# Feed-forward weights narrowed in place; weight remainders and gate products dealt out anew between VectorE and GpSimd

## The chip, the cores and the metric

The kernel runs on one core of a Trainium2 chip. The metric is the device time of one execution, in microseconds (us). The engines are TensorE (PE in the profile, its weight loads PEld), VectorE (DVE), ScalarE (ACT), GpSimd (POOL) and SyncE (SP), which issues most transfers. Each has its own queue of instructions and works through it in a fixed order.

## The reference, cut to what matters

```python
def reference(**kwargs):
    attn_out = _attn_ref(q, k, v, tau)            # 4 batches, 8 heads, 576 tokens, 64 wide
    x = attn_out.transpose(0, 2, 1, 3).reshape(B * S, H * D)        # 2304 x 512
    x = _moe_ref(x=x, **moe_kwargs)               # 8 experts, w1 512 x 1024, w2 1024 x 512
    return _moe2_ref(x=x, **moe2_kwargs)

def _moe_ref(x, expert_emb, tau, w1, w2):
    ...
    for e in range(E):                            # each token goes to its best expert
        h = np.maximum(x[mask] @ w1[e], 0.0)
        out[mask] = gate_w[mask, None] * (h @ w2[e])

def _moe2_ref(x, w_in, w_out):                    # w_in 512 x 2048, w_out 2048 x 512, as float64
    h = x @ w_in
    sp = np.where(h > 20.0, h, np.log1p(np.exp(np.minimum(h, 20.0))))
    return (h * np.tanh(sp) @ w_out).astype(np.float32)
```

## The kernel before

**Stages.** The attention with the router fills the first 298 us. Then come eight visits, called experts 0 to 7 here (`visit`, L984), in which the tokens of an expert are gathered and go through its two products, up to about 565 us. The feed-forward runs in five groups of token columns (2, 4, 4, 4, 4 blocks) to the end.

**Split products.** Each f32 operand of a product is held as a high part, rounded to the type that TensorE takes, and a remainder. A product is three matmuls: high by high, low by high, high by low. So each operand costs a cast on ACT (`xh`, `wh`, `hi`) and a subtraction (`xl`, `wl`, `lo`). For the hidden tiles the subtraction is L1067 on DVE (`lo`), for the gathered rows L1044 on DVE (`xl`), for the experts' weights L960 (`wl`), on DVE or on POOL by the table `PR2['split']`. An expert's weights are four quarters of 128 x 2048 (`raw`, 1 MB each), and each quarter is cast and subtracted in two halves of 1024 columns.

**A visit.** `fetch` (L962) gathers 128 token rows with their gate from DRAM (L966, on POOL's queue) into one of three buffers `q32` and multiplies them by the gate, which stands in a column beside the row (on ACT at L971). PE transposes them (L1037), four matmuls each, with `ident`. The first product (L1061) makes eight hidden tiles u = 0 to 7, each with its `hi` and `lo`; the next expert's transposes stand between the seventh and the eighth tile. The second product (L1084) takes the `hi` and `lo` of all eight. The first expert's first 256 rows are done ahead of the rest (`early_part`), while `dispatch` and `places` (L773 to L879) work out where every token goes, in some 60 small operations on DVE.

**Narrowing.** The feed-forward's weights lie in DRAM as float64. `ffn_narrow` (L1208) turns them into f32 in 32 pieces of 128 x 512. A piece is loaded into `fraw` (512 KB, two buffers). ACT scales its high words into `b`. DVE makes in `c` the low word shifted right by 29 (L1221, the shift count being a second operand `by29`), puts the sign to it (L1222), then adds `b` shifted left by three (L1225). `c` (two buffers) is stored to DRAM. Before the feed-forward `ffn_weights` (L1239) reads the pieces back (L1251), casts them (L1253, ACT) and subtracts (L1257, DVE or POOL).

**What sets the order.** Every step is an operation of a planner (`Plan.add`), with an engine, an assumed duration, a priority (`prio`) and an assumed delay until its result can be used (`lat`). `Plan.order` simulates the engines by these numbers and writes down an order for each of them; the priorities come from the tables `PR` and `PR2`. An engine doesn't leave this order at run time: if the instruction at its head waits, all behind it wait.

Of the kernel before, what the change touches and what calls it, by code (L numbers as in the profile page):

```python
# [7 lines left out]
F32 = mybir.dt.float32  # L8
# [3 lines left out]
U32 = mybir.dt.uint32  # L12
# [24 lines left out]
PR = {'er': -15.54, 'ep': 12.91, 'ep2': 5.77, 'route': 119.01, 'route2': 74.91, 'rkpos': 41.48, 'rkpos2': 8.02, 'S': -59.65, 'max': -521.82, 'exp': 48.0, 'stt': -105.97, 'thr': 8.58, 'T': 9.58, 'Tp': 199.57, 'Tc': -0.63, 'TL': 10.76, 'TLp': 55.36, 'TLc': -285.26, 'pv': 19.05, 'x': -3.47, 'po': 66.46, 'osb': -13.34, 'px': 210.03, 'xev': 161.57, 'rd': 140.54, 'scale': 121.08, 'load': -59.04, 'xsc': 97.82, 'Ts': 2.12, 'xpos': 10.54, 'early': 270.81, 'h0': 16.86, 'h1': 9.87, 'h2': 34.96, 'h3': 47.14, 'rk3': 10.38, 'rk4': 11.04, 'tp3': 62.39}  # L37
PR2 = {'f0': (103, 153, 152, 184), 'pipe': (), 'dve_hi': (0, 5, 6), 'xo': 24.33, 'ps': (9.4, 19.4), 'cd': 1048576.0, 'split': (('ACT', 'DVE'), ('ACT', 'DVE'), ('ACT', 'POOL'), ('ACT', 'POOL'), ('ACT', 'DVE'), ('ACT', 'DVE'), ('ACT', 'POOL'), ('ACT', 'DVE')), 'sl': 28000, 'll': 2000, 'pool_lo': (0, 2, 5, 7), 'gbuf': 4, 'lag': 897.0, 'fw': 842.14, 'fw_act': (0, 1, 2, 3), 'fw_pool': (1, 3), 'n0': 0, 'n1': 0.46, 'np': 396.93, 'ld': -414.26, 'w0': -38.7, 'w1': -307.33, 'wlo': 327.12, 'xg': -219.77, 'xt': -641.51, 'xh': -523.34, 'h': -520.32, 'hs': -813.02, 'ht': -471.8, 'hh': -463.67, 'yy': -39.15, 'ye': 28.32, 'yi': 894.81, 'fy': 292.37, 'ft': 292.4, 'fx': 257.19, 'f1': -828.67, 'sg': -63.24, 'rc': 593.64, 'gg': 101.32, 'gh': -7.22, 'gl': -102.51, 'ob': -951.49, 'pt': -761.98, 'acc': 3.98}
# [212 lines left out]
class Kernel:  # L251
# [76 lines left out]
    def consts(self):  # L328
# [38 lines left out]
        self.by29 = c("by29", [128, 1], U32)  # L367
# [27 lines left out]
        def weights():  # L395
# [12 lines left out]
            g.iota(self.by29, pattern=[[0, 1]], base=29, channel_multiplier=0)  # L408
# [569 lines left out]
    def put(self, v, d, o, y, n, dst, prio, after):  # L978

        nc, add = self.nc, self.pl.add  # L980
        add("ACT", t_act(n), lambda: nc.scalar.copy(y()[:, 0:n], o()[:, 0:n]), r=[o], w=[y], prio=prio - 800)  # L981
        return add("SP", 600, lambda: nc.sync.dma_start(dst(), y()[:, 0:n]), r=[y, "off"], w=[("y", v, d)], prio=prio, lat=2000, dma=512.0 * n, after=after)

    def visit(self, v):  # L984
# [12 lines left out]
        for c in range(4):  # L997
# [7 lines left out]
            add("SP", 600, load, r=["reg"], w=[rt], prio=T - 200 + c if v else 100 + c, lat=2000, dma=PR2["cd"])  # L1005
# [19 lines left out]
        for k in range(k0, k0 + n):  # L1025
# [3 lines left out]
            self.fetch(self.ids[:, j:j + 1], self.x_dram[:, :], need, xg, -600 + T + 10 * k, "ACT")  # L1029
# [112 lines left out]
    def overflow(self, i):  # L1142
# [26 lines left out]
        R = [h("b", 0), h("b", 1), h("c", 0), h("c", 1)]  # L1169
# [38 lines left out]
    def ffn_narrow(self, n, i, at, raw, e, w, keys, after=()):  # L1208
# [5 lines left out]
        kr, ke, kw = keys  # L1214
        add("SP", 600, lambda: nc.sync.dma_start(raw(src.dtype), src[:, s]), w=[kr], prio=at - 4, lat=2000, dma=524e3, after=after)
# [43 lines left out]
    def ffn_rows(self, gi):  # L1259
# [223 lines left out]
```

## Time and profile before

| | |
|---|---|
| median of 3 runs | 988.83 us (988.18 to 992.61) |
| the profiled execution | 993.31 us |
| its span, first to last instruction | 991.6 us |
| PE busy | 926.2 us, 93% |
| DVE busy | 745.3 us, 75% |
| ACT busy | 569.3 us, 57% |
| POOL busy | 341.5 us, 34% |
| mean clock granted to PE | 0.979 |

The profile shows one execution. Busy time says how long an engine worked, not what the end waited for. For that one reads, stage by stage, how much PE lacks of the stage, which instructions ended its waits, and then what stood ahead of those instructions on their own engine. A row of waits sums the idle time of an engine just before an operation and names what released it. The granted clock is the share of TensorE's full speed in a stretch.

### The profile page before, as it was taken

The page shows a single profiled execution, that of the slowest core. Times are in us where ns is not written, and L with a number is a line of the kernel's source. Part 1 is how long each engine was busy: PE and PEld are TensorE (multiplying, and loading weights), DVE is VectorE, ACT ScalarE, POOL GpSimd, SP SyncE. Part 2 cuts the span into 40 slices and gives each one's busy share as a digit, 9 for nine tenths or more (in the row PEclk, how much of TensorE's full clock was granted, in tenths as well). Part 3 has the DMA queues.
Part 4 walks back from the last instruction along what each step waited for, and adds up shares of the span by engine and source line. Part 5 has one row for each costly group of instructions (what it writes and reads, how often), then busy time and mean ns, then how long its engine had stood idle before and what let it go on. Part 6 is the DMA issues. An engine that isn't in the chain of part 4 may idle for free. (4 is left out here: it accounts for less than half of the span.)

```text
span 991.6 us, 17464 instructions
## 1 busy us (share of the span) xinstructions
PE 926.2 (93%) x6574; PEld 740.6 (75%) x6574; DVE 745.3 (75%) x1023; ACT 569.3 (57%) x933; POOL 341.5 (34%) x429
## 2 busy tenths in 40 slices
PE   5899999999899898998989998999999999999997
PEld 3456555555568888998989996788888888888885
DVE  6888988888839586977894775994859495775972
ACT  3778887777765544555555673552635354443551
POOL 4333333333215222413333642332433233324223
PEclk7999999999999998999999899999999999999999
DMA  4122423323324778988878540100100001000001
GB/s 151 59 94 92 131 80 123 99 82 119 134 88 170 257 271 297 296 319 306 285 282 273 184 146 3 43 22 22 43 22 22 21 1 43 1 1 22 21 1 43
DMA packets 45637, 115.73 MB, mean 117 GB/s; under 512 B 11029, under 2 KB 16170, under 8 KB 41450
## 3 DMA queue, kind: packets, MB, share of 16 engines
q1 hardware_dynamic: 42426, 104.30, 31.2%
q0 software_dynamic: 3120, 10.25, 2.9%
q8 instruction: 54, 0.88, 0.4%
q14 instruction: 37, 0.30, 0.1%
HBM read 91.55 MB, written 22.97 MB: 115 GB/s over the span
## 5 line engine op out<-in xcount | busy, mean ns | idle before, releaser
L1340 DVE RECIPROCAL p<-p 128x512 f32<-128x512 f32 x72 | 241.0, 3347 | 100.6 <-ACT p L1336 100.6
L1345 POOL TENSOR_TENSOR lo<-p,hi 128x512 fp32r<-128x512 f32 x72 | 92.9, 1293 | 180.2 <-ACT hi L1344 101.1
L511 PE MATMUL D<-QK 64*128 64x288 f32 (+1 forms) x640 | 107.1, 457 | 21.1 <-DVE P L518 10.6
L517 ACT ACTIVATE E<-D,m 128x576 f32<-128x576 f32 x144 | 103.9, 742 | 37.3 <-DVE m L515 32.6
L515 DVE TENSOR_REDUCE m<-D 128x1 f32<-128x576 f32 x144 | 104.2, 750 | 16.2 <-PE D L511 16.0
L518 DVE SCALAR_TENSOR_TENSOR P<-D,thr,E 128x576 f32<-128x576 f32 x128 | 101.5, 812 | 15.0 <-ACT E L517 14.3
L960 POOL TENSOR_TENSOR wl<-raw,wh 128x1024 fp32r<-128x1024 f32 x24 | 62.7, 2628 | 107.1 <-ACT wh L958 106.6
L538 ACT COPY T<-D 128x1024 f32<-128x1024 f32 (+1 forms) x80 | 74.2, 929 | 29.4 <-PE D L535 28.8
L1344 ACT CAST hi<-p 128x512 fp32r<-128x512 f32 x72 | 44.0, 610 | 78.8 <-PE S L1352 42.6
L1084 PE MATMUL B<-lo,wh 128*128 128x256 f32 (+3 forms) x256 | 79.5, 311 | 8.6 <-DVE lo L1067 8.6
L516 POOL TENSOR_SCALAR thr<-m,ntau 128x1 f32<-128x1 f32 x144 | 38.6, 271 | 134.7 <-DVE m L515 116.9
L569 PE MATMUL D<-T,V 128*64 128x512 f32 x320 | 83.5, 608 | 0.9 <-DVE P L518 0.5
L1061 PE MATMUL S<-xh,wh 128*128 128x256 f32 (+3 forms) x256 | 78.7, 307 | 3.8 <-DVE lo L1067 3.6
L511 PEld LDWEIGHTS D<-QK 64*128 64x128 f32 (+1 forms) x640 | 47.2, 183 | 45.7 <-issue 18.4
L1084 PE MATMUL B<-hi,wh 128*128 128x256 f32 (+3 forms) x256 | 79.2, 309 | 1.5 <-ACT osb L981 0.9
L1061 PE MATMUL S<-xl,wh 128*128 128x256 f32 (+3 forms) x256 | 78.0, 304 | 2.4 <-DVE xl L1044 2.4
L1084 PE MATMUL B<-hi,wl 128*128 128x256 f32 (+3 forms) x256 | 78.8, 308 | 0.0
L1061 PE MATMUL S<-xh,wl 128*128 128x256 f32 (+3 forms) x256 | 78.1, 305 | 0.0
L958 ACT CAST wh<-raw 128x1024 fp32r<-128x1024 f32 x64 | 64.2, 1053 | 7.9 <-DMA raw<-in_wm_dram 4.0
L960 DVE TENSOR_TENSOR wl<-raw,wh 128x1024 fp32r<-128x1024 f32 x40 | 57.5, 1466 | 10.8 <-ACT wh L958 8.2
L1334 ACT ACTIVATE p<-S 128x512 f32<-128x512 f32 x36 | 21.5, 597 | 68.2 <-PE S L1326 52.1
L1084 PEld LDWEIGHTS B<-lo,wh 128*128 128x128 f32 x256 | 51.5, 201 | 10.1 <-DVE lo L1067 10.1
(296 smaller groups left out, 2308.4 us busy)
## 6 DMA issues: line engine op xcount, KB each, us to landing
raw<-in_wm_dram SPq DMA_DIRECT2D x32, 1024.0 KB, 7.9
QK<-in_qk_dram SPq DMA_DIRECT2D x32, 432.0 KB, 4.2
V<-in_v_dram SPq DMA_DIRECT2D x16, 512.0 KB, 3.2
fraw<-in_w_in_dram SPq DMA_DIRECT2D x16, 512.0 KB, 7.1
fraw<-in_w_out_dram SPq DMA_DIRECT2D x16, 512.0 KB, 5.0
x_dram<-xs SPq DMA_DIRECT2D x16, 256.0 KB
w_in_dram<-c SPq DMA_DIRECT2D x16, 256.0 KB
w_out_dram<-c SPq DMA_DIRECT2D x16, 256.0 KB, 5.3
```

The source lines that it names most:

```text
L511: nc.tensor.matmul(o, lhsT=QK()[r, a, q0:q0 + w], rhs=QK()[r, a, S:], start=True, stop=True)
L515: add("DVE", 680, lambda: nc.vector.tensor_reduce(m(), sv(), axis=AX.XY, op=ALU.max, negate=True), r=[sc], w=[m], prio=at + PR["max"])
L517: add("ACT", 660, lambda: nc.scalar.activation(Ev(), sv(), AF.Exp, bias=m(), scale=1.0), r=[sc, m], w=[E], prio=at + PR["exp"])
L518: add("DVE", 750, lambda: nc.vector.scalar_tensor_tensor(outs[0]().rearrange("p (a b) -> p a b", a=2), sv(), thr(), Ev(), op0=ALU.is_ge, o ...
L538: add("ACT", (2 * w + 100) / 1.2, lambda: nc.scalar.copy(T()[:, :, 0:w], pt()[:, :, 0:w]), r=[pt], w=[T], prio=at + PR["Tc"])
L569: mul = lambda j, o, c, rhs: nc.tensor.matmul(o, lhsT=V1()[:, c, :], rhs=rhs, start=(a == 0), stop=(a == 4))
L958: add("ACT", t_act(1024, False), lambda: nc.scalar.copy(hi()[:, s], raw()[:, s]), r=[kr], w=[kh], prio=prio, fill=fill)
L960: add(le, d, lambda: e.tensor_tensor(lo()[:, s], raw()[:, s], hi()[:, s].bitcast(F32), op=ALU.subtract), r=[kr, kh], w=[kl], prio=prio + . ...
L1061: hd(nc.tensor.matmul(hp(), lhsT=a()[:, kc, f], rhs=x()[:, kc, cols], start=(i == 0), stop=(i == 11)))
L1084: nc.tensor.matmul(o()[:, 0:N_], lhsT=w[a]()[:, u % 4, 128 * d:128 * (d + 1)], rhs=H2[x], start=(u == 0 and i == 0), stop=(u == 7 and i == 2))
L1340: v.reciprocal(q_(), q_())
L1345: add("POOL", t_pool(512), lambda q_=q_, gh=gh, gl=gl: g.tensor_tensor(gl(), q_(), gh().bitcast(F32), op=ALU.subtract), r=[q_, gh], w=[gl] ...
```

## The change

1. **Narrowing in place.** The shift writes back into `fraw` and takes its count as a number (one tensor operand). The sign is put to it there. The third operation writes into `b`, and `b` is what is stored. The tile `c` and the constant `by29` go; `b` has four buffers in place of two each of `b` and `c`, and where the feed-forward used two `b` and two `c` as result rows it uses four `b`. `fraw` is read until the third operation; before, the second was the last to read it.
2. **Remainders of the experts' weights** (`PR2['split']`, pairs for the two halves of quarters 0 to 3). Before, from the second expert on: DVE DVE, POOL POOL, DVE DVE, POOL DVE. After: POOL POOL, DVE DVE, DVE POOL, DVE POOL. The first expert's first quarter stays on DVE. In all 34 of the 64 on DVE, which had 40, and 30 on POOL, which had 24.
3. **Gate products of gathered rows**: on POOL for all experts but the first, 17 instructions of 128 x 512; before, all on ACT.
4. **The planner's numbers**: longer delays for the result store, the weight loads, the narrowing's loads and stores and the reading back, a shorter one between a stored piece and its reading, and some priorities. They change only the orders.

```diff
...
-'split': (('ACT', 'DVE'), ('ACT', 'DVE'), ('ACT', 'POOL'), ('ACT', 'POOL'), ('ACT', 'DVE'), ('ACT', 'DVE'), ('ACT', 'POOL'), ('ACT', 'DVE')), 'sl': 28000
+'split': (('ACT', 'POOL'), ('ACT', 'POOL'), ('ACT', 'DVE'), ('ACT', 'DVE'), ('ACT', 'DVE'), ('ACT', 'POOL'), ('ACT', 'DVE'), ('ACT', 'POOL')), 'sl': 2000
...
-            add("SP", 600, load, r=["reg"], w=[rt], prio=T - 200 + c if v else 100 + c, lat=2000, dma=PR2["cd"])
+            add("SP", 600, load, r=["reg"], w=[rt], prio=T - 200 + c if v else 100 + c, lat=7500 if v else 4000, dma=PR2["cd"])
...
-            self.fetch(self.ids[:, j:j + 1], self.x_dram[:, :], need, xg, -600 + T + 10 * k, "ACT")
+            self.fetch(self.ids[:, j:j + 1], self.x_dram[:, :], need, xg, -600 + T + 10 * k, "POOL" if v else "ACT")
...
-        R = [h("b", 0), h("b", 1), h("c", 0), h("c", 1)]
+        R = [h("b", x) for x in range(4)]
...
-        def low():
-            v.tensor_tensor(w(), words(U32, 0), self.by29.to_broadcast([128, 512]), op=ALU.logical_shift_right)
-            v.scalar_tensor_tensor(w(), words(U32, 1), 0x80000000, w(), op0=ALU.bitwise_and, op1=ALU.bitwise_or)
-
-        add("DVE", 690 + 690, low, r=[kr], w=[kw], prio=at)
-        add("DVE", 690, lambda: v.scalar_tensor_tensor(w(), e().bitcast(U32), 3, w(), op0=ALU.logical_shift_left, op1=ALU.bitwise_or), r=[ke], w=[kw], prio=at)
-        x = add("SP", 600, lambda: nc.sync.dma_start(self.f_dram[n][:, s], w().bitcast(F32)), r=[kw], w=[("f0", n, i)], prio=at, lat=2000, dma=262e3)
+        kt = (kr, "t")
+        add("DVE", 560, lambda: v.tensor_scalar(words(U32, 0), words(U32, 0), 29, None, op0=ALU.logical_shift_right), r=[kr], w=[kt], prio=at)
+        add("DVE", 690, lambda: v.scalar_tensor_tensor(words(U32, 0), words(U32, 1), 0x80000000, words(U32, 0), op0=ALU.bitwise_and, op1=ALU.bitwise_or), r=[kr, kt], w=[kt], prio=at)
+        add("DVE", 690, lambda: v.scalar_tensor_tensor(e().bitcast(U32), e().bitcast(U32), 3, words(U32, 0), op0=ALU.logical_shift_left, op1=ALU.bitwise_or), r=[kt, ke], w=[ke], prio=at)
+        x = add("SP", 600, lambda: nc.sync.dma_start(self.f_dram[n][:, s], e()), r=[ke], w=[("f0", n, i)], prio=at, lat=8000, dma=262e3)
...
```

Lines move up by two in `visit` and by four behind the narrowing, so that L1067 is L1065 after the change, L960 is L958, and L966 is L964. The orders of all engines are unchanged up to the end of the attention. Three places behind it follow.

On DVE, in the first product of expert 1, the second visit (128x384), where `lo` is the remainder of a hidden tile, `wl` that of the next expert's weights, and `c`, `fraw` and `b` belong to the narrowing. Before:

```order
L1067 SCALAR_TENSOR_TENSOR lo<-S,hi 128x384
L960 TENSOR_TENSOR wl<-raw,wh 128x1024 x2
L1067 SCALAR_TENSOR_TENSOR lo<-S,hi 128x384 x2
L1221 TENSOR_TENSOR c<-fraw,by_119 128x512
L1222 SCALAR_TENSOR_TENSOR c<-fraw,c 128x512
L1225 SCALAR_TENSOR_TENSOR c<-b,c 128x512
L1067 SCALAR_TENSOR_TENSOR lo<-S,hi 128x384
L1044 TENSOR_TENSOR xl_6791<-S,xh_6761 128x4x128 x3
L1221 TENSOR_TENSOR c<-fraw,by_119 128x512
L1222 SCALAR_TENSOR_TENSOR c<-fraw,c 128x512
L1067 SCALAR_TENSOR_TENSOR lo<-S,hi 128x384
```

After:

```order
L1221 SCALAR_TENSOR_TENSOR b<-b,fraw 128x512
L1065 SCALAR_TENSOR_TENSOR lo<-S,hi 128x384 x4
L1219 TENSOR_SCALAR fraw<-fraw 128x512
L1220 SCALAR_TENSOR_TENSOR fraw<-fraw 128x512
L1065 SCALAR_TENSOR_TENSOR lo<-S,hi 128x384
L1221 SCALAR_TENSOR_TENSOR b<-b,fraw 128x512
L1042 TENSOR_TENSOR xl_6766<-S,xh_6736 128x4x128 x3
L1219 TENSOR_SCALAR fraw<-fraw 128x512
L1220 SCALAR_TENSOR_TENSOR fraw<-fraw 128x512
L1065 SCALAR_TENSOR_TENSOR lo<-S,hi 128x384
```

The rows begin with the fourth `lo` before and with the third after. The pair of remainders behind the fourth `lo` went to another place, and four `lo`s now follow on each other. Ahead of the last `lo` two operations of the narrowing stand in both.

On POOL, at the gathers for experts 0 to 2; q32 with a number is one buffer's use, L964 the gather and L967 the gate product, L958 the remainder. Before:

```order
L966 DMA q32_5902<-x_dram_92,ids_156 128x514
L966 DMA q32_5909<-x_dram_92,ids_156 128x514
L966 DMA q32_5955<-x_dram_92,ids_156 128x514
L960 TENSOR_TENSOR wl_5830<-raw_5233,wh_5818 128x1024
L960 TENSOR_TENSOR wl_5988<-raw_5887,wh_5970 128x1024
L966 DMA q32_6025<-x_dram_92,ids_156 128x514
L966 DMA q32_6047<-x_dram_92,ids_156 128x514
L966 DMA q32_6056<-x_dram_92,ids_156 128x514
L966 DMA q32_6144<-x_dram_92,ids_156 128x514
L966 DMA q32_6173<-x_dram_92,ids_156 128x514
```

After:

```order
L964 DMA q32_5882<-x_dram_92,ids_155 128x514
L964 DMA q32_5894<-x_dram_92,ids_155 128x514
L964 DMA q32_5900<-x_dram_92,ids_155 128x514
L958 TENSOR_TENSOR wl_5908<-raw_5259,wh_5823 128x1024
L964 DMA q32_5994<-x_dram_92,ids_155 128x514
L967 TENSOR_SCALAR q32_5900<-q32_5900 128x512
L964 DMA q32_6031<-x_dram_92,ids_155 128x514
L964 DMA q32_6057<-x_dram_92,ids_155 128x514
L958 TENSOR_TENSOR wl_6028<-raw_5903,wh_6021 128x1024
L967 TENSOR_SCALAR q32_5994<-q32_5994 128x512
L964 DMA q32_6136<-x_dram_92,ids_155 128x514
L967 TENSOR_SCALAR q32_6031<-q32_6031 128x512
```

The gate products stand between the gathers now, one gather late: the product of q32_6031 comes behind the gather of q32_6136. The three buffers go round, so that this gather writes where q32_5994 was, whose transposes on PE stand directly ahead of those of q32_6031.

On DVE, in the first product of the last expert (128x192). Before:

```order
L960 TENSOR_TENSOR wl<-raw_8994,wh 128x1024 x2
L960 TENSOR_TENSOR wl<-raw,wh 128x1024
L1067 SCALAR_TENSOR_TENSOR lo<-S,hi 128x192 x4
L1257 TENSOR_TENSOR raw_9388<-raw_9388,raw 128x512
L1067 SCALAR_TENSOR_TENSOR lo<-S,hi 128x192
L1257 TENSOR_TENSOR raw_9388<-raw_9388,raw 128x512
L1067 SCALAR_TENSOR_TENSOR lo<-S,hi 128x192 x2
L1257 TENSOR_TENSOR wl<-wl,wh 128x512
L1067 SCALAR_TENSOR_TENSOR lo<-S,hi 128x192
```

After:

```order
L1065 SCALAR_TENSOR_TENSOR lo<-S,hi 128x192
L1253 TENSOR_TENSOR xl_9100<-xl_9100,xh_9182 128x512
L1065 SCALAR_TENSOR_TENSOR lo<-S,hi 128x192 x2
L1219 TENSOR_SCALAR fraw<-fraw 128x512
L1065 SCALAR_TENSOR_TENSOR lo<-S,hi 128x192
L1220 SCALAR_TENSOR_TENSOR fraw<-fraw 128x512
L1065 SCALAR_TENSOR_TENSOR lo<-S,hi 128x192
L1221 SCALAR_TENSOR_TENSOR b<-b,fraw 128x512
L1219 TENSOR_SCALAR fraw<-fraw 128x512
L1065 SCALAR_TENSOR_TENSOR lo<-S,hi 128x192
L1220 SCALAR_TENSOR_TENSOR fraw<-fraw 128x512
L1065 SCALAR_TENSOR_TENSOR lo<-S,hi 128x192
```

Before, no piece was narrowed here; now the narrowing's operations alternate with the `lo`s.

## Rows read from the trace of the kernel before

**Rows 1.** Stages: length; busy us of PE, PEld, DVE, ACT, POOL; clock, DMA share, GB/s.

```profile
298.00:345.00 47.00, 42.81 (x271) 38.47 (x271) 34.27 (x79) 24.47 (x42) 18.56 (x13) 0.96 0.58 211
345.00:545.00 200.00, 183.47 (x1255) 180.53 (x1254) 156.12 (x187) 109.19 (x184) 63.61 (x32) 0.97 0.85 291
545.00:625.00 80.00, 72.11 (x486) 64.98 (x485) 55.56 (x45) 44.50 (x85) 35.45 (x25) 0.94 0.35 110
625.00:992.00 367.00, 359.91 (x1565) 293.50 (x1563) 259.65 (x132) 170.58 (x288) 121.65 (x114) 0.99 0.06 21
```

**Rows 2.** PE's waits, 298 to 640 us: total us, times, longest.

```profile
PE B L1084 <- DVE lo L1067: 8.6, 5, 2.4
PE S L1037 <- DVE lo L1067: 4.3, 4, 2.1
PE S L1061 <- DVE lo L1067: 3.6, 2, 2.2
...
PE S L1061 <- DVE xl L1044: 2.4, 1, 2.4
...
PE S L1037 <- ACT q L971: 1.3, 1, 1.3
```

**Rows 3.** Stretches of 10 us with a lower granted clock, columns as in Rows 1.

```profile
320.00:330.00 10.00, 7.36 (x43) 6.77 (x42) 5.10 (x17) 2.83 (x7) 3.44 (x3) 0.83 0.87 323
370.00:380.00 10.00, 7.92 (x38) 7.82 (x38) 7.73 (x12) 4.39 (x7) 3.54 (x4) 0.83 1.00 376
380.00:390.00 10.00, 7.63 (x35) 7.42 (x34) 8.91 (x9) 4.08 (x8) 4.30 (x2) 0.83 0.64 185
...
530.00:540.00 10.00, 7.84 (x53) 7.63 (x52) 7.13 (x11) 5.69 (x11) 2.14 (x2) 0.83 0.83 292
```

**Rows 4.** Timeline 378 to 384 us: start, us, engine, line; in brackets idle before.

```profile
379.15 5.16 POOL L960 TENSOR_TENSOR wl<-raw,wh 128x1024 fp32r<-128x1024 f32 x2 [5.20 <-ACT wh L958]
...
379.32 2.75 DVE L1222 SCALAR_TENSOR_TENSOR c<-fraw,c 128x512 uint32<-128x512 uint32 x1
...
382.58 0.44 PE L1084 MATMUL B<-lo,wh 128*128 128x384 f32 x1 [2.37 <-DVE lo L1067]
```

**Rows 5.** Timeline 367 to 374 us, DVE and PE.

```profile
368.73 2.35 DVE L960 TENSOR_TENSOR wl<-raw,wh 128x1024 fp32r<-128x1024 f32 x2
...
372.08 0.66 PE L1037 MATMUL S<-ident,q 128*128 128x128 f32 x4 [2.11 <-DVE lo L1067]
```

**Rows 6.** DVE's groups from 298 us: busy us, mean ns, idle before by releaser.

```profile
L960 DVE TENSOR_TENSOR wl<-raw,wh 128x1024 fp32r<-128x1024 f32 x40 | 57.5, 1466 | 10.8 <-ACT wh L958 8.2 <-issue 2.6
L1222 DVE SCALAR_TENSOR_TENSOR c<-fraw,c 128x512 uint32<-128x512 uint32 x32 | 38.7, 1210 | 1.1
L1225 DVE SCALAR_TENSOR_TENSOR c<-b,c 128x512 uint32<-128x512 uint32 x32 | 27.2, 851 | 1.3
...
L1221 DVE TENSOR_TENSOR c<-fraw,by 128x512 uint32<-128x512 uint32 x32 | 26.0, 812 | 23.8 <-DMA w_in_dram<-c 12.9 <-DMA w_out_dram<-c 10.9
```

**Rows 7.** POOL's groups over the span, columns as in Rows 6.

```profile
L1345 POOL TENSOR_TENSOR lo<-p,hi 128x512 fp32r<-128x512 f32 x72 | 92.9, 1293 | 180.2 <-ACT hi L1344 101.1 <-PE S L1352 51.1 <-issue 12.0
L960 POOL TENSOR_TENSOR wl<-raw,wh 128x1024 fp32r<-128x1024 f32 x24 | 62.7, 2628 | 107.1 <-ACT wh L958 106.6 <-issue 0.5
...
L468 POOL TENSOR_SCALAR QK<-QK 128x288 f32<-128x288 f32 x31 | 28.9, 934 | 21.7 <-DMA QK<-in_qk_dram 18.6 <-PE D L535 3.0
```

**Rows 8.** Timeline 367 to 376 us, POOL.

```profile
371.10 0.94 POOL L966 DMA_INDIRECT q<-x_dram,ids  x1 [0.30 <-issue]
```

**Rows 9.** DVE's groups: a copy before, a PSUM operation after 298 us.

```profile
L450 DVE COPY EB<-ident 64x256 f32<-64x256 f32 x2 | 0.6, 284 | 0.0
...
L1341 DVE SCALAR_TENSOR_TENSOR p<-p,S 128x512 f32<-128x512 f32 x36 | 24.7, 687 | 1.5
```

**Rows 10.** Timeline 311 to 323 us, DVE and POOL.

```profile
313.26 5.33 DVE L863 TENSOR_TENSOR tl<-tl,ge 128x8 f32<-128x8 f32 x1
...
313.87 4.69 POOL L960 TENSOR_TENSOR wl<-raw,wh 128x1024 fp32r<-128x1024 f32 x2
```

More of the change, by code (lines that the diff above doesn't have):

```diff
@@ L38 @@
[L38 removed]
+PR = {'er': -15.54, 'ep': 12.91, 'ep2': 5.77, 'route': 119.01, 'route2': 74.91, 'rkpos': 41.48, 'rkpos2': 8.02, 'S': -59.65, 'max': -521.82, 'exp': 48.0, 'stt': -105.97, 'thr': 8.58, 'T': 9.58, 'Tp': 199.57, 'Tc': -3.64, 'TL': 10.76, 'TLp': 50.91, 'TLc': -285.26, 'pv': 19.05, 'x': -3.47, 'po': 66.48, 'osb': -13.34, 'px': 210.03, 'xev': 161.57, 'rd': 123.62, 'scale': 121.08, 'load': -59.04, 'xsc': 97.82, 'Ts': 2.12, 'xpos': 10.54, 'early': 245.34, 'h0': 16.86, 'h1': 9.87, 'h2': 34.96, 'h3': 30.12, 'rk3': 10.38, 'rk4': 11.53, 'tp3': 64.2}
@@ new lines @@
+PR2 = {'f0': (103, 154, 152, 184), 'pipe': (), 'dve_hi': (0, 5, 6), 'xo': 24.33, 'ps': (9.4, 19.4), 'cd': 1048576.0, 'split': (('ACT', 'POOL'), ('ACT', 'POOL'), ('ACT', 'DVE'), ('ACT', 'DVE'), ('ACT', 'DVE'), ('ACT', 'POOL'), ('ACT', 'DVE'), ('ACT', 'POOL')), 'sl': 2000, 'll': 2000, 'pool_lo': (0, 2, 5, 7), 'gbuf': 4, 'lag': 915.82, 'fw': 842.14, 'fw_act': (0, 1, 2, 3), 'fw_pool': (1, 3), 'n0': 0, 'n1': 0.46, 'np': 396.93, 'ld': -414.26, 'w0': -38.7, 'w1': -307.33, 'wlo': 327.12, 'xg': -219.77, 'xt': -641.51, 'xh': -523.34, 'h': -520.32, 'hs': -813.02, 'ht': -471.8, 'hh': -463.67, 'yy': -39.15, 'ye': 28.32, 'yi': 894.81, 'fy': 292.37, 'ft': 292.4, 'fx': 257.06, 'f1': -828.77, 'sg': -63.24, 'rc': 593.49, 'gg': 101.32, 'gh': -7.67, 'gl': -102.51, 'ob': -951.49, 'pt': -761.98, 'acc': 3.98}
@@ L981, in put @@
         add("ACT", t_act(n), lambda: nc.scalar.copy(y()[:, 0:n], o()[:, 0:n]), r=[o], w=[y], prio=prio - 800)
-        return add("SP", 600, lambda: nc.sync.dma_start(dst(), y()[:, 0:n]), r=[y, "off"], w=[("y", v, d)], prio=prio, lat=2000, dma=512.0 * n, after=after)
+        return add("SP", 600, lambda: nc.sync.dma_start(dst(), y()[:, 0:n]), r=[y, "off"], w=[("y", v, d)], prio=prio, lat=6000, dma=512.0 * n, after=after)
     def visit(self, v):
@@ L1155, in h @@
                 make = {"S": self.big, "B": self.bank}.get(kind, lambda at: self.row(kind, at))
-                if kind in "bc":
-                    make = lambda at: self.h("f", kind, [128, 512], F32 if kind == "b" else U32, 2, at)
+                if kind == "b":
+                    make = lambda at: self.h("f", "b", [128, 512], F32, 4, at)
                 keep[key] = make(at)
@@ L1204, in overflow, with ffn_narrow @@
         self.put_ids(self.idto[i:i + 1, :], lambda: self.id_dram[bass.ds(self.off, 128), :], K("idto"), T + 6)
-    def ffn_narrow(self, n, i, at, raw, e, w, keys, after=()):
+    def ffn_narrow(self, n, i, at, raw, e, keys, after=()):
         nc, add = self.nc, self.pl.add
@@ L1234, in narrow_late @@
             raw = self.h("f", "fraw", [128, 2 * YW], F32, 2, at)
-            e, w = self.h("f", "b", [128, 512], F32, 2, at), self.h("f", "c", [128, 512], U32, 2, at)
+            e = self.h("f", "b", [128, 512], F32, 4, at)
             j = x * PR2["n1"]
-            self.ffn_narrow(n, i, 200 + 10 * j + PR2["np"], lambda dt, raw=raw: raw()[:, 0:1024].bitcast(dt), e, w, [raw, e, w], [marks[min(int(j), SURE - 1)]])
+            self.ffn_narrow(n, i, 200 + 10 * j + PR2["np"], lambda dt, raw=raw: raw()[:, 0:1024].bitcast(dt), e, [raw, e], [marks[min(int(j), SURE - 1)]])
     def ffn_weights(self, n, c, at, tags):
@@ L1270, in ffn_rows @@
             X = [(self.row("hi", ah + .2 * x), self.row("lo", ah + .2 * x)) for x in range(2)]
-            X += [(h("f", "b", [128, 512], F32, 2, ah + x), h("f", "c", [128, 512], U32, 2, ah + x)) for x in range(2)]
+            X += [tuple(h("f", "b", [128, 512], F32, 4, ah + x + y) for y in (0, .5)) for x in range(2)]
         else:
```

9 lines of the change are left out of this document (3 added, 6 removed).

## The prediction

> **What bounds the kernel now.** I read first how busy each engine is by stage [rows 1]. In the last 367 us TensorE (PE) works 359.9 us, so nothing that the other engines save there can shorten it. In the three stages before, it lacks 4.2 of 47, 16.5 of 200 and 7.9 of 80 us, and no other engine is full: VectorE (DVE) is nearest with 156.1 of 200. So PE waits for single results, not for an engine's total. The view of PE's waits names them [rows 2]: 8.6 + 4.3 + 3.6 = 16.5 us end with DVE's `lo` (line 1067, the remainder of a hidden tile), 2.4 us with `xl` (line 1044), 1.3 us with the gate product on ScalarE (ACT, line 971). Third, the clock: in the stretches where PE had such a wait of some 2 us, the mean granted clock is 0.83 instead of 1 [rows 3], that is, a part of each at 1.2 instead of 2.4 GHz. A stretch of 10 us at 0.83 does 8.3 us of full-speed work, so each costs about 1.7 us beyond the wait: one such row in the first stage, three (5.1 us) in the second.
>
> Why is `lo` late? It is itself short. Two patterns stand ahead of it. One: two whole weight remainders (2.35 us) run on DVE just before `lo`, and PE waits 2.11 us [rows 5]. Two: POOL begins a pair of remainders at 379.15, DVE's second narrowing operation, started at 379.32, takes 2.75 us instead of 0.69, and `lo` behind it comes late; PE waits 2.37 us [rows 4]. An undisturbed DVE operation of that size with one tensor in PSUM takes 0.687 us [rows 9]. The five waits under B L1084 are mostly this second pattern, repeated in the next experts.
>
> **The change part by part.** The instruction orders are the same up to 298 us, and the work after 625 us is the same and bound by PE: 0 for both, and 0 for the constant that goes.
>
> *First experts, 298 to 345 us.* In the dispatch a DVE operation of 8 elements takes 5.33 us while POOL runs two remainders [rows 10]; the `xl` behind it are late and PE waits 2.4 us, with one slow stretch: 4.1 us together. After the change only one remainder stands between POOL's gathers there, and `xl` stands ahead of the last remainder on DVE, not behind it. That can free up to 4.1. Against it: on POOL the gate product of row q_6031 now stands behind the gather of q_6136, and that gather must wait until PE has transposed q_5994, whose buffer it takes. PE transposes q_5994 and q_6031 in one go. So PE waits for issue 0.30 + gather 0.94 [rows 8] + the gate product. No row shows this product on POOL. The lower end is POOL's subtraction of the same size, 1.29 us; a POOL multiplication by a per-row number over 288 columns takes 0.934, and by columns 512 would take 1.66; the upper end is the remainder of 1024 columns, 2.63 [rows 7]. I take 1.66, the nearest kind. The wait is 2.9 us (2.5 to 3.9) in place of the 1.3 [rows 2]: +1.6, and probably a slow stretch of 1.7. Net -4.1 + 1.6 + 1.7 = **-0.8** (from -2.9, with no slow stretch, to +4.3 with the dispatch wait still there). The later gate products have cover: a row gathered at 371.10 us [rows 8] goes into the buffer that the transposes of about that time have left, and is itself transposed only near the end of the next expert's first product, so I cost these products at nothing on PE; without that cover each costs up to its 1.66.
>
> *Experts 1 to 6, 345 to 545 us.* Six remainders leave DVE for POOL: 6 x 1.47 = 8.8 us less there [rows 6]. It matters where they stood: the order of DVE shows that the pair of remainders in the middle of expert 1's first product is gone from between its `lo`s. Pattern one should go. Pattern two is only half gone: the last `lo` of expert 1 still stands behind the first two narrowing operations; what changed is which quarter of the weights POOL takes, the first in place of the second, so its pair runs earlier, beside other DVE work. The narrowing's waits for its stores (12.9 + 10.9 us on DVE, the row of line 1221 in [rows 6]) were on DVE's queue but mostly before nothing urgent; longer latencies in the planner put them later. I take half of the 16.5 us: **-8** (from 0 to -14), and half of the slow stretches, **-2.5** (0 to -5.1).
>
> Of the narrowing itself: three operations per piece as before, 96 in all. The first has now one tensor in SBUF instead of two operands. Its price lies between twice a 256-column copy, 0.57 us [rows 9], and today's mean with disturbance, 0.812 [rows 6]; I take 0.69, which saves 32 x 0.12 = 4 us of DVE, part of the slack above and not a term of its own. In place, the raw buffer is held for one operation more, 0.7 to 0.85 us per piece and some more where that operation waits; the next load starts that much later, but the loads may now run on into expert 7, so I cost this at 0 for PE up to expert 6. The page "VectorE: DVE Perf Modes" of the Trainium skill (section "Mode 2×_2P") states that a one-source operation between SBUF tensors can run two elements per cycle; by it the shift would be near half of 0.69 and save a further 11 us of DVE, again off the path. No row of this kernel shows it at this size.
>
> *Last experts and the start of the feed-forward, 545 to 625 us.* The narrowing ended before expert 6; now some 10 of 32 pieces come after the first `lo` of expert 5, 6 of them among the `lo`s and remainders of experts 6 and 7. Six pieces are 18 x 0.69 = 12 us in a stage where DVE works 55.6 of 80 us [rows 1]. It fits by total, but each `lo` there may find one such operation ahead of it, and the feed-forward's weights are read back later. Today's PE loss there is 7.9 us; I take **+3** (0 to +8).
>
> Sum: -0.8 - 8 - 2.5 + 3 = **-8.3 us**. The profiled execution took 993.31 us (span 991.6), so it would be 985.0; the median of the runs is 988.83, 4.5 below the profiled one, and the forecast against it is 988.83 - 8.3 = **980.5 us**.
>
> **The rivals.** *The end gives it back (0.20).* The gains up to expert 6 are as above, but DVE is what the last two experts wait for: the +3 becomes its upper end +8, with one more slow stretch of 1.7. 980.5 + 5 + 1.7 = **987.2**. For it: half the DVE queue between the last `lo`s is narrowing now. Against: 55.6 + 12 of 80 is not full.
>
> *POOL stands in DVE's way (0.15, slower).* POOL gets 6 remainders (6 x 2.63 = 16 us) and 17 gate products (17 x 1.66 = 28 us) on top of 62.7 us of remainders [rows 7]. Today those 62.7 us stretch DVE's two-tensor operations by 32 x (1.21 + 0.85 + 0.81 - 3 x 0.69) = 26 us, and by 40 x (1.47 - 1.37) = 4 us in the remainders [rows 6, 9]: 0.48 us per us of POOL. 44 us more would add 21 us to DVE; if as much of it reaches PE as today's 16.5 of 30, that is +11.6, less some 3 for the remainders that left DVE: 988.83 + 8.6 = **997.4**. It decides once clearly more than the present eleven `lo`s [rows 2] stand behind a stretched operation. For it: rows 4, and the narrowing is spread further among the `lo`s. Against: the gate product reads POOL's own row for 1.66 us, shorter than a remainder pair's 5.2, and the three gates of an expert come right after gathers, when DVE is between products. The page "SBUF — State Buffer" of the Trainium skill (section "Who interferes with whom") speaks for this rival: a DVE instruction with two SBUF inputs contends with a GpSimd instruction that reads SBUF, and a one-source `tensor_scalar` in a two-port mode is blocked too. The 2.75 us against 0.687 agree with its first half; its second half, by which the new shift is no safer than the old, no run here shows, and it would take away the 4 us above.
>
> *The waits only change places (0.10).* PE waits for another `lo`, moved by a few us, as often: the terms -8 and -2.5 are nothing, and 988.83 - 0.8 + 3 = **991.0** is left, no change.
>
> **How the numbers follow.** Forecast 0.55; rivals 0.20, 0.15, 0.10. By over 0.5% (4.9 us, about what a measurement of this kernel can tell from no change) faster is below 983.9: most of the forecast and a little of the first rival, 0.58. Within: 0.25. Slower, above 993.8: the second rival and the bad ends of the first, 0.17. The range runs from the better half of the second stage's bound (-8.3 - 11 = -20: 969) to just beyond no change (994), leaving out most of the second rival and the very best ends. The likeliest case alone runs from 972 to 985.
>
> **What would show it.** Right: PE's waits for `lo` between 345 and 545 us fall from about 16 to 8, with fewer stretches at 0.83; the dispatch operation of 8 elements is no longer 5 us; a new PE wait of about 3 us ends with a gate product on POOL between 325 and 345 us; DVE's busy time from 545 to 577 us grows by about 10. Wrong: DVE's second and third narrowing operations with higher means than 1.21 and 0.85 and PE's waits for `lo` above 16 us (POOL in the way); PE waits for `lo` or for weights read back after 545 us above 8 us (the end). If the last 367 us change by more than 2 us, my zero there is wrong.

## The result

The changed kernel takes **979.26 us** (median of 10 runs, 973.64 to 985.0) against 988.5 us (median of 10 runs of the kernel before). The ratio is 0.990, 95% interval 0.9867 to 0.9934: 6.5 to 13.1 us faster, clear of no change. The forecast was 980.5 us.

The profiled execution has a span of 972.5 us against 991.6. That is twice what the medians differ by: the profiled execution of before is near the top of its kernel's runs and that of after near the bottom of its own. So the two traces show where time goes, while amounts are taken from the runs.

The experts' second product on PE bounds the stretch in which the gain lies. In the view of one line, with count, shortest/median/longest ns and first and last start, before and after:

```profile
L1084 PE MATMUL B<-hi,wh x256: 269/283/522, 342.7 to 575.4; 128*128 128x256 f32 x48, 128*128 128x192 f32 x32, 128*128 128x384 f32 x32, 128*128 128x320 f32 x16
```

```profile
L1082 PE MATMUL B<-hi,wh x256: 272/283/415, 338.6 to 557.2; 128*128 128x256 f32 x48, 128*128 128x192 f32 x32, 128*128 128x384 f32 x32, 128*128 128x320 f32 x16
```

From its first to its last start it took 232.7 us and takes 218.6, 14.1 less. From its last start to the end of the span it is 416.2 and 415.3, nearly the same. Its first start is 4.1 us earlier after the change, but 3.4 us of that are there already at the end of the attention, where both kernels run the same instructions in the same order, so they are no effect of the change.

To compare stages they have to be cut at the same work. The first row of each pair goes from the first start of the second product in expert 0 to that in expert 6, the second from there to its last start in expert 7; columns as in [rows 1]. Before:

```profile
342.70:537.30 194.60, 178.07 (x1211) 175.13 (x1211) 157.17 (x188) 106.47 (x178) 58.73 (x29) 0.96 0.85 291
537.30:575.40 38.10, 36.64 (x287) 36.13 (x286) 22.69 (x26) 24.49 (x50) 24.11 (x14) 0.91 0.57 188
```

After:

```profile
338.60:513.30 174.70, 170.02 (x1211) 169.23 (x1211) 138.95 (x163) 95.86 (x160) 100.98 (x49) 1.00 0.85 297
513.30:557.20 43.90, 36.33 (x288) 35.55 (x287) 37.71 (x43) 24.89 (x51) 23.37 (x13) 0.92 0.81 268
```

Up to expert 6 the same work takes 19.9 us less: PE lacks 4.7 us of its stretch instead of 16.5, and its granted clock is 1.00 instead of 0.96. The last expert gives 5.8 us of that back: PE lacks 7.6 us there instead of 1.5, and DVE has 37.7 us of work where it had 22.7. POOL works 101.0 us in the first stretch where it worked 58.7. PE's waits after, 297 to 640 us, as in [rows 2]:

```profile
PE S L1035 <- POOL q L967: 5.5, 3, 3.5
PE S L1059 <- DVE lo L1065: 4.5, 1, 4.5
PE B L1082 <- DVE lo L1065: 3.7, 3, 1.9
...
PE S L1035 <- POOL wl L958: 1.3, 1, 1.3
```

The waits for `lo` fell from 16.5 us in eleven to 8.2 in four, and 5.5 us for gate products on POOL are new. Cut at expert 6, the waits for `lo` are 15.6 + 0.9 us before and 1.5 + 6.7 after: they are nearly gone up to expert 6, and new ones stand in the last expert. In total it looks as the prediction had it. The experiments say otherwise of the cause.

### The profile page after: what moved, and what is told of

It is laid out like the page before. It is cut to its first block, busy times and chain, and to the rows that moved or that the text cites. A ratio compares the mean times of both kernels' runs of the same rounds, so it can differ in the third digit from the quotient of the medians.

```text
span 972.5 us, 17460 instructions
## 1 busy us (share of the span) xinstructions
PE 914.5 (94%) x6574; PEld 734.0 (75%) x6574; DVE 739.8 (76%) x1017; ACT 559.1 (57%) x916; POOL 393.3 (40%) x451
## 5 line engine op out<-in xcount | busy, mean ns | idle before, releaser
L513 DVE TENSOR_REDUCE m<-D 128x1 f32<-128x576 f32 x144 | 104.3, 752 | 16.5 <-PE D L509 16.5
L958 POOL TENSOR_TENSOR wl<-raw,wh 128x1024 fp32r<-128x1024 f32 x30 | 78.5, 2631 | 60.0 <-ACT wh L956 58.2
L1082 PE MATMUL B<-lo,wh 128*128 128x256 f32 (+3 forms) x256 | 76.4, 298 | 3.7 <-DVE lo L1065 3.7
L1082 PE MATMUL B<-hi,wh 128*128 128x256 f32 (+3 forms) x256 | 76.3, 298 | 0.9 <-ACT osb L979 0.9
L1082 PE MATMUL B<-hi,wl 128*128 128x256 f32 (+3 forms) x256 | 76.0, 297 | 0.0
L958 DVE TENSOR_TENSOR wl<-raw,wh 128x1024 fp32r<-128x1024 f32 x34 | 55.5, 1662 | 15.6 <-ACT wh L956 14.8
L1348 PE MATMUL S<-wh,hi 128*128 128x512 f32 x144 | 56.9, 395 | 2.7 <-ACT hi L1340 2.5
```

Of the source, the lines that this page charges most:

```text
L513: add("DVE", 680, lambda: nc.vector.tensor_reduce(m(), sv(), axis=AX.XY, op=ALU.max, negate=True), r=[sc], w=[m], prio=at + PR["max"])
L958: add(le, d, lambda: e.tensor_tensor(lo()[:, s], raw()[:, s], hi()[:, s].bitcast(F32), op=ALU.subtract), r=[kr, kh], w=[kl], prio=prio + . ...
L1082: nc.tensor.matmul(o()[:, 0:N_], lhsT=w[a]()[:, u % 4, 128 * d:128 * (d + 1)], rhs=H2[x], start=(u == 0 and i == 0), stop=(u == 7 and i == 2))
L1348: ad(t, nc.tensor.matmul(acc(t), lhsT=a()[:, k], rhs=x, start=(u == 0 and f == 0 and n == 0), stop=(u == 16 // fw - 1 and f == fw - 1 and ...
```

## The experiments

Theory A is that of the prediction: the gain comes from where the remainders run and stand. Its rivals: the planner's numbers bring it (B), or the narrowing in place, which the prediction had counted at nothing (C). Ratios are to the kernel before on the same chip, with 95% intervals.

### One part at a time

**e1_numbers**: the kernel before with the new numbers of the planner alone, for instance

```diff
-            add("SP", 600, load, ..., lat=2000, dma=PR2["cd"])
+            add("SP", 600, load, ..., lat=7500 if v else 4000, dma=PR2["cd"])
```

> The kernel before with the planner's new delays and priorities alone: no new split, gate products on ACT, narrowing through c. Theory A (the gain comes from where the weight remainders run and stand): little, 984 to 990 us, since six more remainders stay on DVE and the pairs still stand among the hidden-tile remainders. Rival B (the new delays and priorities do it by themselves): 978 to 982, and PE's waits for lo between 345 and 545 us fall below 8 us as in the changed kernel.

Measured: 987.85 us, ratio 1.0015 (0.9987 to 1.0043). No change, so B falls as an account of the gain. But in its trace, cut as above, this zero looks like the sum of two effects:

```profile
339.40:522.90 183.50, 177.93 (x1251) 176.37 (x1251) 144.77 (x176) 106.38 (x181) 58.02 (x29) 0.99 0.87 301
522.90:569.10 46.20, 38.55 (x288) 37.76 (x286) 40.13 (x43) 25.72 (x51) 23.62 (x14) 0.85 0.77 258
```

Up to expert 6 it is 11.1 us shorter than before, and 8.1 us longer behind it (one execution each, and that of before is 4.8 us above its median). The long last expert goes with these numbers: its stretch is 42 to 46 us in the three kernels that have them (this one, the changed one and e4), and 34 to 40 in all the others but e11 (45.6).

**e2_in_place**: the kernel before with the narrowing of the changed kernel (its three operations, the store from `b`, four buffers `b`) and nothing else.

> The kernel before with the narrowing in place alone (with four b buffers), old numbers, old split, gates on ACT. Theory A: 986 to 990, no change, since the shift's 0.42 us in place of 0.69 saves some 8 us of DVE off the path and the raw buffer is held longer. Rival C (DVE's saved time is the gain): 980 or less, and PE's waits for lo fall by half.

Measured: **974.29 us, 0.9883 (0.9847 to 0.9919)**. This part alone brings what the whole change brings, and its last expert is not longer:

```profile
341.30:518.10 176.80, 171.79 (x1211) 170.43 (x1210) 141.84 (x184) 106.28 (x178) 59.37 (x29) 0.99 0.87 314
518.10:552.90 34.80, 33.57 (x287) 32.85 (x286) 23.85 (x28) 24.68 (x51) 24.26 (x14) 1.00 0.71 240
```

PE's waits for `lo` are down to 5.5 us:

```profile
PE S L1059 <- DVE lo L1065: 2.5, 2, 2.0
...
PE S L1035 <- DVE lo L1065: 1.7, 3, 1.2
PE B L1082 <- DVE lo L1065: 1.3, 1, 1.3
```

**e3_split_gates**: the kernel before with the new `PR2['split']` and the gate products of all experts but the first on POOL.

> The kernel before with the new split of remainders and the gate products on POOL alone, old numbers and narrowing through c. Theory A: 979 to 985, most of the gain; pairs of remainders are gone from between the hidden-tile remainders, and PE's waits for lo between 345 and 545 us fall by 5 us or more. Rivals B and C: 988 to 995, because POOL's 44 us more of reads stretch DVE's two-tensor operations (second narrowing operation above a mean of 1.21 us) and nothing pays for it.

Measured: 999.74 us, 1.0127 (1.0087 to 1.0168), slower. Theory A falls. Of the 988.5 us that is +12.5, where the prediction's rival "POOL stands in DVE's way" had +8.6. The two runs that follow take it apart.

**e7_split**: the kernel before with the new split alone.

```diff
-'split': (('ACT', 'DVE'), ('ACT', 'DVE'), ('ACT', 'POOL'), ...
+'split': (('ACT', 'POOL'), ('ACT', 'POOL'), ('ACT', 'DVE'), ...
```

> The kernel before with the new split of the weight remainders alone. My first theory said that this brings the gain (979 to 985), which e3 speaks against. Rival now: 16 us more of POOL's remainders stretch DVE, and the pairs on POOL come at a worse place: 989 to 997.

Measured: 1000.01 us, 1.0096 (1.0063 to 1.0128). The split, from which the prediction expected the gain, costs 1% by itself. Its trace shows where, in PE's waits:

```profile
PE S L1037 <- DVE lo L1067: 19.1, 5, 4.8
```

In five of the experts PE now waits up to 4.8 us at the next rows' transposes; such waits were 4.3 us in four in [rows 2]. All five have one pattern, here in expert 1: POOL runs a pair of remainders beside the last tiles of the first product, and two narrowing operations that stand between the `lo`s take 2.4 to 2.9 us each under it, where 0.69 is undisturbed.

```profile
365.14 5.71 POOL L960 TENSOR_TENSOR wl<-raw,wh 128x1024 fp32r<-128x1024 f32 x2 [3.88 <-ACT wh L958]
365.84 2.77 DVE L1222 SCALAR_TENSOR_TENSOR c<-fraw,c 128x512 uint32<-128x512 uint32 x1
...
369.01 2.40 DVE L1225 SCALAR_TENSOR_TENSOR c<-b,c 128x512 uint32<-128x512 uint32 x1
...
371.93 2.81 PE L1037 MATMUL S<-ident,q 128*128 128x128 f32 x12 [2.09 <-DVE lo L1067]
```

That is the mechanism of the rival just named, and the +9.5 us are near its price.

**e8_gates**: the kernel before with the gate products on POOL alone.

```diff
-            self.fetch(..., -600 + T + 10 * k, "ACT")
+            self.fetch(..., -600 + T + 10 * k, "POOL" if v else "ACT")
```

> The kernel before with the gate products of all experts but the first on POOL alone. If it is these that made e3 slow: 992 to 1000, with waits of PE that end with a gate product and higher means of DVE's narrowing operations. If they cost what e4 gave back: 987 to 992, and the split has the rest.

Measured: 989.2 us, 1.000 (0.9967 to 1.0032). In total the seventeen POOL operations cost nothing that can be measured here. The trace has 5.3 us of new waits at the transposes, two that the profile puts to no releaser, and 10.9 us of waits for `lo` instead of 16.5.

**e4_gates_on_act**: the changed kernel, planned as it is, but with the gate products executed on ACT.

```diff
-            add("POOL", 2200, lambda: g.tensor_scalar(xg()[:, 0:DM], ..., gate(), None, op0=ALU.mult), ...
+            add("POOL", 2200, lambda: nc.scalar.activation(xg()[:, 0:DM], ..., AF.Copy, scale=gate()), ...
```

> The changed kernel with every engine's order as it is, only the 17 gate products executed on ACT at their place in time. It prices the gates on POOL. If POOL's reads cost PE much (rival: POOL in DVE's way), 33 us less of them give 970 to 975 and DVE's narrowing operations have lower means (third below 0.9 us). If they are hidden, only the waits of PE that end with a gate product go (5.5 us in the trace, of which ACT's products would give some back): 974 to 978.

Measured: 974.9 us, 0.9875 (0.9841 to 0.991). That is within the interval of e2, and the changed kernel's own interval overlaps it: the gates on POOL may cost some 0.25%, but the runs don't settle it. PE's waits for gate products on POOL are gone; at the same transposes 1.3 us end with a gate product on ACT, and 8.2 us with `lo`.

Put together: in place 0.988, numbers 1.0015, split 1.0096, gates 1.000. One after the other these would give 0.999, and the change measures 0.990. So the parts don't add up: beside the narrowing in place, split and numbers together cost nothing (e4 against e2), while the split costs 1% in the old plan. No run has split and numbers together without the narrowing in place.

### What of the narrowing in place is it?

It differs from the old form in several things: the shift has one tensor operand; the pieces have four buffers `b`; shift and sign are planned as two operations; no piece waits on DVE for a store; and the raw buffer is held until the third operation. One run each for the first four.

**e5_two_operands**: e2 with the shift's count as a second operand again.

```diff
-v.tensor_scalar(words(U32, 0), words(U32, 0), 29, None, op0=ALU.logical_shift_right)
+v.tensor_tensor(words(U32, 0), words(U32, 0), self.by29.to_broadcast([128, 512]), op=ALU.logical_shift_right)
```

> The narrowing in place alone, as in e2, but the shift takes its count as a second operand again, as before the change; DVE's order is that of e2. It prices the form of the shift: 0.43 us against 0.69 in e2's trace, some 32 x 0.26 = 8 us of DVE. Theory D (the gain of e2 is DVE's time ahead of the lo's): back to 981 to 987. Theory E (the gain is the four buffers and the order): stays at 973 to 978.

Measured: 973.8 us, 0.9851 (0.9801 to 0.9901). The shift then takes a mean of 0.967 us instead of 0.616, 11 us more of DVE in all, and the time is the same. DVE's time is not the gain.

**e6_two_buffers**: e2 with two buffers `b` for the pieces.

```diff
-            e = self.h("f", "b", [128, 512], F32, 4, at)
+            e = self.h("f", "b", [128, 512], F32, 2, at)
```

> The narrowing in place alone, as in e2, but with two buffers b for the pieces instead of four (the feed-forward's other two result rows have a ring of their own); DVE's order is that of e2. Theory E (four buffers): DVE or ACT waits for the stores again, some 20 us as before, and the time goes back to 982 to 988. Theory D: stays at 973 to 978.

Measured: **967.15 us, 0.9775 (0.9722 to 0.9827)**, the fastest of all, ahead of both kernels. Four buffers are not the gain. In the same 200 us as the second of [rows 1] PE works 193.3 us at full clock where it worked 183.5 at 0.97 (e2 has 193.8 there):

```profile
345.00:545.00 200.00, 193.26 (x1401) 191.45 (x1401) 154.95 (x201) 121.68 (x208) 75.02 (x38) 1.00 0.86 304
```

DVE's order up to 640 us is the same in e2, e5 and e6. What makes e6 the faster of them isn't told by any run: the profiled executions took 970.21 us in e6 and 970.82 in e2, so the traces don't hold the difference.

**e9_lo_first**: the kernel before, with shift and sign moved from between an expert's last two `lo`s to right behind the last, wherever they stood there.

```diff
...
+                    if when[self.los[v, k0, 6]] < when[x] < when[i]:
+                        moved[x] = when[i] + 1e-3
...
```

> The kernel before with one thing moved: where the first two narrowing operations stand between the last two lo's of an expert on DVE, they now stand right behind the last one. Theory G (a second narrowing operation that is caught by POOL's pair of remainders just ahead of the last lo is what costs): PE's waits for lo in the second product (8.6 us in five) fall below 3 us, a stretch or two of slow clock go with them: 976 to 983. If other waits take their place: 985 to 990.

Measured: 989.37 us, 1.0034 (1.0004 to 1.0064), no gain. This removes the second pattern of the prediction, and the waits in the second product do go, from 8.6 to 0.2 us. But:

```profile
PE S L1049 <- DVE lo L1079: 7.6, 6, 2.1
PE S L1073 <- DVE lo L1079: 6.0, 4, 3.8
...
PE B L1096 <- DVE lo L1079: 0.2, 1, 0.2
```

The transposes and the first product wait 13.6 us for other `lo`s, where [rows 2] had 7.9. The late operation of [rows 4] was a place where delay came to light; moving it out of the way moved the waits.

**e10_three_c**: the kernel before with three buffers `c`.

```diff
-            e, w = ..., self.h("f", "c", [128, 512], U32, 2, at)
+            e, w = ..., self.h("f", "c", [128, 512], U32, 3, at)
```

> The kernel before with three buffers c instead of two, so that a piece no longer waits on DVE for the store of the piece but one before it (23.8 us of DVE's waits). Theory H (the in-place form gains because it takes that wait off DVE's queue): DVE's waits for these stores fall below 8 us and the time to 974 to 982. Theory G: 984 to 990, as the second operation still stands ahead of the last lo.

Measured: 987.33 us, 0.9988 (0.9963 to 1.0013), no change. The waits for stores on DVE, 23.8 us in [rows 6], are gone, and waits for the loads, 19.1 us, stand in their place (e2 has 26.5 us of them, and the gain):

```profile
DVE c L1221 <- DMA fraw<-in_w_in_dram: 12.4, 5, 4.2
DVE c L1221 <- DMA fraw<-in_w_out_dram: 6.7, 5, 2.5
```

**e11_three_units**: the kernel before, planned with shift and sign as two operations.

```diff
-        add("DVE", 690 + 690, low, r=[kr], w=[kw], prio=at)
+        add("DVE", 560, lambda: v.tensor_tensor(w(), words(U32, 0), self.by29...), r=[kr], w=[kw], prio=at)
+        add("DVE", 690, lambda: v.scalar_tensor_tensor(w(), words(U32, 1), 0x80000000, w(), ...), r=[kr], w=[kw], prio=at)
```

> The kernel before, with the tile c and its buffers, but planned with the shift and the sign as two operations, as the in-place form has it. If the gain of e2 is the order that the planner finds with smaller units: 970 to 979. If it is what the buffers wait for (theory H): 984 to 990.

Measured: 995.56 us, 1.0092 (1.0058 to 1.0125), slower. **e12_in_place_two_units** is the other half, e6 with shift and sign planned as one operation.

```diff
...
+            v.tensor_scalar(words(U32, 0), words(U32, 0), 29, None, op0=ALU.logical_shift_right)
+            v.scalar_tensor_tensor(words(U32, 0), words(U32, 1), 0x80000000, words(U32, 0), ...)
+        add("DVE", 690 + 690, low, r=[kr], w=[kt], prio=at)
...
```

> The narrowing in place with two buffers as in e6, but planned with shift and sign as one operation, as before the change; DVE's order is then nearly that of the kernel before. If the gain is what the buffers wait for: 964 to 974 as e6. If it is the order of smaller units: 980 to 988.

Measured: 975.6 us, 0.9868 (0.9824 to 0.9911). Smaller units are not the gain either, though e6, which has them, is 0.9% faster with intervals that just meet. PE's waits for `lo` in e12 are those of an in-place kernel, 7.3 us:

```profile
PE B L1082 <- DVE lo L1065: 3.2, 4, 2.1
PE S L1059 <- DVE lo L1065: 2.1, 2, 1.8
PE S L1035 <- DVE lo L1065: 2.0, 1, 2.0
```

**What is shown and what stays open.** All four kernels that narrow in place and keep the old split are 1.2 to 2.3% faster; all seven that keep `c` are at 0.999 to 1.013. So the in-place form brings the gain by itself; whether the rest of the change could bring it without that form, no run shows. What does it within the form is not the shorter shift (e5), not the four buffers (e6), not the planner's smaller units (e11, e12), and the wait for the stores alone doesn't do it (e10). What is left untried is that the raw buffer is held to the third operation, and that the planner, which knows that, puts loads, ACT's scaling and DVE's operations at slightly other places: in e2's expert 1, for one, the third operation stands behind the last but one `lo` where before it stood ahead of it. No run takes these two apart. ACT's waits for raw pieces fit at first sight (33.0 us before, 17 to 27 in the four in-place kernels, 34 to 52 in e9, e10 and e11), but in e1 they are 6.3 us without any gain, so that isn't it alone. It stays open.

## Why the prediction was right, and where it wasn't

**The number was right and most of its reason was wrong.** That the total came out at 980.5 is luck: the prediction had -8 and -2.5 us from the split and nothing from the narrowing in place, and the runs have about -11.6 from the narrowing and, beside it, nothing from the split and the numbers (e4 against e2).

- *The split (the reason for most of the -8 in experts 1 to 6).* Alone it is +9.5 us (e7: 0.96% of 988.5). The step that failed is that POOL's pair now "runs earlier, beside other DVE work". In e7 that work is the narrowing between the `lo`s, and PE waits 19.1 us for it. In the changed kernel the pair of expert 1 runs beside `lo`s that follow on each other, and they take 0.5 us each all the same:

```profile
359.39 5.10 POOL L958 TENSOR_TENSOR wl<-raw,wh 128x1024 fp32r<-128x1024 f32 x2 [3.88 <-ACT wh L956]
359.78 1.48 DVE L1065 SCALAR_TENSOR_TENSOR lo<-S,hi 128x384 fp32r<-128x384 f32 x3
```

- *The narrowing in place ("part of the slack above and not a term of its own").* This is the step that failed most: it should have been a term of about -11.6 us (e2: 1.17% of 988.5). The prediction costed the operations, 4 us of DVE, and looked for their cover; e5 shows that their duration indeed doesn't matter. It saw that the raw buffer is held for one operation more and took that as a later load, at 0. What it didn't ask is what this and the missing `c` do to the plan of all engines.
- *The waits and the clock.* Half of the 16.5 us of waits were to go, and 8.2 are left, but not where it said: up to expert 6 nearly all go (15.6 to 1.5), and 6.7 stand in the last expert. Likewise half of the slow stretches were to go there and none is left (clock 1.00). In the two traces that stretch is 19.9 us shorter, where the forecast was 10.5; the traces differ by twice what the runs do. Between 345 and 545 us the kernel before had four slow stretches and not three: one lies across two of the rows that [rows 3] cut, from 455 to 465 us, at 0.83.
- *The dispatch and the gate queue (-0.8).* Counted from the same product of the first expert's early rows (start at 297.95 before and 294.57 after), the first start of the second product comes 44.75 us later before and 44.03 after, 0.7 us less. The 2.4 us wait of `xl` is gone, and the 8-element operation of [rows 10] with its 5.33 us too, though another of 8 elements now takes 3.05. The gate's new wait is where it was forecast, behind the gather:

```profile
325.77 1.03 POOL L964 DMA_INDIRECT q<-x_dram,ids  x1 [1.73 <-PE S L1035]
326.83 3.12 POOL L967 TENSOR_SCALAR q<-q 128x512 f32<-128x512 f32 x2
```

```profile
328.47 1.07 PE L1035 MATMUL S<-ident,q 128*128 128x128 f32 x4 [3.46 <-POOL q L967]
```

It took 3.46 us (forecast 2.9, from 2.5 to 3.9). A queue inverted by the order can be read and priced before the run.

- *The price of the gate product.* Taken as 1.66 us; it is 1.73 in the median and longer where DVE stands in its way:

```profile
L967 POOL TENSOR_SCALAR q<-q x17: 1555/1726/3381, 315.7 to 470.5; 128x512 f32<-128x512 f32 x17
```

- *"The later gate products have cover"* failed at one place: a product queued behind a remainder, and PE waits 1.86 us at 462.07.

```profile
457.33 2.40 POOL L958 TENSOR_TENSOR wl<-raw,wh 128x1024 fp32r<-128x1024 f32 x1 [1.88 <-ACT wh L956]
459.72 2.25 POOL L967 TENSOR_SCALAR q<-q 128x512 f32<-128x512 f32 x1
```

- *The end (+3, from 0 to +8).* It is there, mis-sized within its bounds: 5.8 us between the like places above. DVE's work in that stretch grows by 15.0 us (forecast: about 10 between 545 and 577 us). From 540 to 550 us DVE has no idle time, PE waits 4.53 us in one piece, and the granted clock is 0.66, a mix of 2.4 and 1.2 GHz.

```profile
540.00:550.00 10.00, 8.71 (x53) 8.71 (x54) 10.00 (x17) 5.61 (x14) 5.35 (x5) 0.66 0.78 254
```

```profile
541.29 0.53 PE L1059 MATMUL S<-xh,wh 128*128 128x192 f32 x1 [4.53 <-DVE lo L1065]
```

Before, PE's waits in the last expert were 0.86 and 0.56 us. The rival in which the end gives the gain back needed a loss of 9.7 us there; what it costs lies between that and the +3. Without the planner's new numbers, in e2, the end costs nothing.

- *The rival "POOL stands in DVE's way".* In the changed kernel its mechanism came true and its price didn't. In DVE's groups after, against [rows 6]:

```profile
L958 DVE TENSOR_TENSOR wl<-raw,wh 128x1024 fp32r<-128x1024 f32 x34 | 55.5, 1662 | 15.6 <-ACT wh L956 14.8 <-DMA raw<-in_wm_dram 0.7
L1221 DVE SCALAR_TENSOR_TENSOR b<-b,fraw 128x512 uint32<-128x512 uint32 x32 | 33.6, 1050 | 1.8 <-ACT b L1216 0.3 <-DMA raw<-in_wm_dram 0.3
L1220 DVE SCALAR_TENSOR_TENSOR fraw<-fraw 128x512 uint32<-128x512 uint32 x32 | 31.8, 995 | 0.6
L1219 DVE TENSOR_SCALAR fraw<-fraw 128x512 uint32<-128x512 uint32 x32 | 28.0, 875 | 11.3 <-DMA fraw<-in_w_out_dram 10.2 <-DMA fraw<-in_w_in_dram 1.1
```

Taking the shortest of each group as undisturbed (1.21, 0.68, 0.68 and 0.41 us), the stretch is 15 + 12 + 10 + 15 = 52 us, against 37 us before by the same reckoning: 15 us more, where 21 were forecast. The step that failed is "if as much of it reaches PE as today". In the new plan it doesn't: e4 has 49 us of stretch and e2 has 32, at the same time. In the old plan it does: e7 has 46 us and e3 has 41, and they are 9.5 and 12.5 us slower, near the 8.6 of this rival; the five waits of e7 show how. And it is the remainders that stretch DVE, not the gate products: e8, which adds these alone, has 37 us like the kernel before.

- *The rival "the waits only change places"* is what happens in e9 and e10, not in the change as a whole.

## What to carry to other kernels

Where in-order queues are filled by a planner, the view of waits names the operation at which a delay comes to light; taking that operation away (e9) or its wait (e10) moves the delay to the next place. Price each part of a change also by what it makes the planner do to the others (how long a buffer is held, which loads follow), and run the parts alone: here the part that was written off as free brought the whole gain by itself, and the part that looked like the remedy cost 1% by itself. Cut stages at the same work and not at the same time: so cut, the numbers that change nothing in total (e1) take 11.1 us out of one stretch and put 8.1 into the next. A right total is no proof of its terms.

## What the runs showed of the hardware

**The one-source shift is fast and no safer.** The prediction's lower end for it was 0.57 us. Its row after:

```profile
L1219 DVE TENSOR_SCALAR fraw<-fraw x32: 413/425/2646, 336.8 to 544.3; 128x512 uint32<-128x512 uint32 x32
```

In the median it takes 0.425 us, against about 0.69 for the two-operand form (e5), although it steps over every other word: 0.62 of it, where the prediction's estimate was near half. The direction agrees with the page "VectorE: DVE Perf Modes" of the Trainium skill (section "Mode 2×_2P"), which the prediction cited without a row. And it is stopped by POOL as the two-operand form is, here under a remainder of 2.81 us:

```profile
339.65 2.36 DVE L1219 TENSOR_SCALAR fraw<-fraw 128x512 uint32<-128x512 uint32 x1
```

```profile
338.91 2.81 POOL L958 TENSOR_TENSOR wl<-raw,wh 128x1024 fp32r<-128x1024 f32 x1
```

It ends 0.29 us after that remainder. This is the half of the rule of "SBUF — State Buffer" (the Trainium skill, section "Who interferes with whom") that the prediction left open, and this trace agrees with it.

**Both sides pay.** Where two remainders on DVE meet two on POOL, 6.71 us on DVE (2 x 1.21, the shortest) stand beside 6.14 on POOL (2 x 2.36, the shortest):

```profile
532.07 6.14 POOL L958 TENSOR_TENSOR wl<-raw,wh 128x1024 fp32r<-128x1024 f32 x2
```

```profile
532.58 6.71 DVE L958 TENSOR_TENSOR wl<-raw,wh 128x1024 fp32r<-128x1024 f32 x2
```

PE's wait of 4.53 us in the last expert comes behind these two.
